# Two chunks of a gated-recurrence layer loaded together, four tokens to a partition, in a kernel that goes on with a wide MLP

## The chip, the cores and the metric

The kernel runs on one core of a Trainium2 chip. The core has five engines with queues of their own: TensorE (PE; PEld are its weight loads), VectorE (DVE), ScalarE (ACT), GpSimd (POOL) and SyncE (SP, which issues most DMAs). Each executes its queue in order; semaphores make one wait for another. The metric is the device time of one execution in microseconds. Steps that an engine takes are called by the kernel's own names throughout (h0.01, qm3.1 and so on); the section on the kernel explains them.

## The reference

For each of 4 batches and 8 heads a state of 48 x 48 runs over 768 tokens. It is decayed by a gate, grows by an outer product, and is read by q:

```
f = 1 / (1 + exp(-f_logit))
for t in range(S):
    state = f[:, :, t, :, None] * state + einsum('bhd,bhe->bhde', k[:, :, t], v[:, :, t])
    y[:, :, t] = einsum('bhd,bhde->bhe', q[:, :, t], state)
```

The result, 3072 tokens x 384, goes through an MLP with 2048 hidden units whose activation is h times cos(h):

```
h = x @ w_in
out = (h * cos(h)) @ w_out
```

## The kernel before

**Chunks and pairs.** The 768 tokens of a batch are cut into chunks of 128. Two neighbouring chunks make a pair of 256 tokens, loaded and prepared together; there are 12 pairs, three to a batch. In a pair's tile one partition holds two neighbouring tokens, e = 0 and 1, for all 8 heads; partitions 0 to 63 are the first chunk (g = 0) and 64 to 127 the second (g = 1). A load (`load`, L294) therefore reads 2 x 48 floats, 384 bytes, in one piece, and 384 KB in one DMA. Heads are worked on four at a time, u = 0 and 1.

**Steps of a pair n** (function `pair`, L311). f, k, q, v are loaded. ACT makes ex (exp(-f_logit)) and ln (log(1 + that), the negative log of the gate). For most pairs POOL adds the two tokens' logs (ad) and PE sums them over the tokens of a chunk by a triangular matrix (cum, L370; its small matmuls with `half` give the totals of each chunk). ACT makes eb and ei, the decays exp(-sum) and exp(+sum). As one sum serves two tokens, the first token of q and the first of k are corrected by one step: fx and fy (ACT) prepare the factors, qa and ka (POOL) apply them. qm and km (L404) multiply q and k by the decays and write them as bf16 side by side in one tile `qk`. vb casts v, and four vt copies lay v out for the matmuls.

The tile qk is then turned, so that head dimensions come to the partitions: for pairs 0 to 4 by PE (tq, tk, L435, sixteen transposing matmuls a pair) and a copy out of PSUM (qkt), for the pairs of `TURN_QK`, 5 to 11, by two DMAs issued from SP (L424). sc (L456) makes the scores k.q, which are masked on the way out of PSUM by am (DVE, L461, 128 x 1024). For the DMA-turned pairs each score matmul is split into two halves, as the turned layout has the two tokens apart. ps (L479) makes the outer products of k and v for the states; st (DVE, L497) adds the state before and sz (DVE, L503) decays the sum. y (L531) is the part of the output from within a chunk, yi that from the state. xe copies the result, already transposed and in bf16, for the MLP.

Pairs 0 and 1 (`HALVES`) are cut into halves of four heads: their f, k and q come in two DMAs each of 192 KB, ex, ln, fx, cum, eb and ei work on half tiles, the log of the two tokens is added by PE (two matmuls instead of one), and qa and ka run partly on DVE.

**The MLP.** `moe` (L566) works on units of 128, 128 and then eleven times 256 tokens; unit m of 256 tokens is pair m - 1. h (L579) is the first matmul into a tile of two PSUM banks, ph, of 1024 columns: h{m}.{j}{s} is half s of tile j. co (ACT, L584) makes the cosine, g (DVE, L561) the product, and o (L595) the second matmul, four steps o{r}.{0..3} to 128 rows; ot copies to SBUF and out stores. The weights arrive in four quarters each, w0.i and w1.i, 768 KB a DMA, and are cast to bf16 by wc on POOL or ACT.

**Order.** Nothing is scheduled at run time or by the compiler: the string `ORDER` (L36) lists every step with its engine's letter (T = PE, S = ACT, V = DVE, G = POOL, Y = SP) and the slot or the PSUM bank of what it writes. An engine's queue is the list of its own steps in that order. A tile name has a number of slots (`SLOTS`), so a load waits until the slot's last readers are done. The steps zf are `ZEROS` = 54 matmuls of a tile of zeros, 128 x 512, whose result nobody reads; they stand in the first part of PE's queue. The steps zqk, zsp, zsz and zvt clear tiles once.

Of the kernel before, what the change touches and what calls it, by code (L numbers as in the profile page):

```python
# [16 lines left out]
C = 128  # L17
# [19 lines left out]
zvt.2:V zsp.1:V zsp.0:G zsz.3:V f0.1:Y0 f0.0:S zqk.0:G k0.0:Y0 ex0.1:S ex0.0:S k0.1:Y ln0.1:S1  # L37
zf0:T0 zf1:T0 zf2:T0 zf3:T0 zf4:T0 zf5:T0 zf6:T0 zf7:T0 zf8:T0 zf9:T0 cum0.1:T0 ln0.0:S cum0.0:T1
fx0.0:S ei0.1:S0 fx0.1:S ei0.0:S ka0.0:V f1.1:Y1 km0.0:G0 f1.0:Y ex1.1:S ka0.1:V zf10:T2 zf11:T2
zf12:T2 zf13:T2 zf14:T2 zf15:T2 zf16:T2 zf17:T2 tk0.0:T2 eb0.1:S0 ex1.0:S ln1.1:S1 ln1.0:S fx1.0:S  # L40
q0.1:Y0 q0.0:Y v0:Y0 fx1.1:S eb0.0:S qa0.1:V zqk.1:V qm0.1:V vb0:S0 f3:Y2 k1.1:Y1 km0.1:V qa0.0:V
zf18:T3 cum1.1:T3 zf19:T4 zf20:T4 zf21:T4 tq0.1:T0 cum1.0:T1 qm0.0:G zsz.2:G eb1.0:S1 vt0.3:S2
k1.0:Y ei1.0:S0 ex3:S zf22:T4 zf23:T4 zf24:T4 zf25:T4 zf26:T4 ps0.1:T4,5 ps0.0:T tk0.1:T v1:Y1 f2:Y0
qkt0.1:V0 eb1.1:S ln3:S0 ei1.1:S ka1.0:G q1.0:Y0 tq0.0:T ka1.1:G km1.1:G0 zvt.1:G vt0.0:S ad3:G1
vt0.1:G q1.1:Y vb1:S1 qkt0.0:V1 vt0.2:G zsz.1:G ex2:S w0.1:Y0 w0.0:Y1 k3:Y0 q3:Y1 w0.3:Y2 ln2:S1
vt1.2:S1 fy3:S zf27:T6 zf28:T6 zf29:T6 zf30:T6 zf31:T6 zf32:T6 sc0.0:T0 sz0.01:V2 sz0.00:V w0.2:Y3
ad2:G0 vt1.0:G km1.0:V vt1.3:G wc0.1:G am0.0:V0 zf33:T6 zf34:T6 yi0:T4 sc0.1:T2 am0.1:V1 st0.11:V
sz0.11:V3 wc0.0:G k2:Y1 zf35:T6 zf36:T6 zf37:T6 zf38:T6 ps1.1:T6,7 tk1.0:T0 ps1.0:T zf39:T1 zf40:T1
zf41:T1 cum3:T1 fy2:S ei3:S0 fx3:S ka3:G eb3:S2 vt1.1:S fx2:S km3.0:G1 qa3:G qm3.0:G km3.1:G qm3.1:G
w1.0:Y0 qa1.0:V st0.10:V qa1.1:V qm1.0:V wc0.2:G ka2:G q2:Y2 tk1.1:T2 zf42:T3 zf43:T3 y0:T3 tq1.0:T  # L50
xe0.1:S0 sz0.10:V st1.00:V st1.01:V qm1.1:V v2:Y1 zf44:T5 zf45:T5 zf46:T5 zf47:T5 zf48:T5 tq1.1:T
cum2:T1 sz1.00:V1 qkt1.0:V0 eb2:S0 xe0.0:S ei2:S1 qkt1.1:V1 km2.0:G0 km2.1:G zf49:T5 sc1.0:T4
sz1.01:V zf50:T0 zf51:T0 sc1.1:T2 h0.01:T0 st1.11:V sz1.11:V2 am1.1:V0 wc1.0:G qa2:G zf52:T6 zf53:T6
h0.00:T co0.0:S0 qm2.1:G am1.0:V1 h1.01:T2 h1.00:T co1.0:S1 y1:T6,4 yi1:T g0.0:V1 xe1.1:V1 st1.10:V
qm2.0:G vb2:G1 sz1.10:V g1.0:V4 w1.2:Y3 xe1.0:S tk3.0:T5 h2.01:T0 tq3.0:T w1.3:Y0 qkt3.0:V0 v3:Y0
# [6 lines left out]
o3.3:T o0.3:T o2.2:T q4:Y2 ps3.0:T4,5 ps3.1:T zsz.0:G vt2.2:G ad4:G0 yi2:T2,3 y2:T vt3.3:G sz3.01:V0
sz3.00:V o1.3:T cum4:T4 v4:Y0 vt3.0:G ad5:G0 fy4:S eb4:S0 st3.11:V fx4:S k4:Y1 fy5:S qa4:G qm4.0:G1
fx5:S ei4:S1 o0.1:T o2.1:T o3.1:T xe2.0:V1 st3.10:V sz3.10:V1 qm4.1:G sz3.11:V xe2.1:V ot2:V0
h3.00:T2 o1.1:T cum5:T0 ei5:S0 eb5:S2 k5:Y0 h3.01:T ot0:V1 vb4:G0 ka4:G y3:T4,5 yi3:T q5:Y1 h3.10:T0
h3.11:T co3.0:S0 xe3.0:V0 xe3.1:V ot1:V2 ot3:V3 co3.1:S2 g3.0:V4 h3.21:T4 h3.20:T co3.2:S1 h4.21:T6
h4.20:T g3.1:V ka5:G km4.0:G co4.2:S0 km4.1:G vt4.1:G2 qa5:G h4.11:T2 h4.10:T g3.2:V co4.1:S2
h4.31:T0 k6:Y2 qm5.1:G0 h4.30:T vt4.0:G vt4.2:G km5.1:G f6:Y1 v5:Y0 v6:Y1 f7:Y0 tq4.0:T4 tq4.1:T5
out3:Y tk4.0:T tk4.1:T co4.3:S1 g4.2:V2 h3.31:T6 h3.30:T qkt4.1:S0 qkt4.0:V1 g4.1:V o5.1:T4 co3.3:S0
o5.2:T o5.0:T o4.1:T5 g4.3:V g3.3:V ps4.1:T0,1 ps4.0:T st4.01:V st4.00:V sc4.1:T2 sc4.0:T6 am4.1:V0  # L70
am4.0:V1 sz4.00:V0 sz4.01:V qm5.0:G vt4.3:G st4.10:V tq5.1:Y2 sz4.10:V2 o5.3:T o4.2:T km5.0:G o4.0:T
o4.3:T ex6:S ln6:S0 vb6:G0 ad6:G0 ex7:S cum6:T2 y4:T3,6 tq5.0:Y3 yi4:T ot5:S3 st4.11:V sz4.11:V
# [116 lines left out]
def describe(nc, cpool, ppool, q, k, v, f_logit, moe_w_in, moe_w_out, out):  # L189
# [528 lines left out]
```

## Time and profile before

| what | value |
|---|---|
| median of 3 runs | 183.36 us (182.91 to 183.54) |
| the profiled execution, its own time | 183.05 us |
| its span, first to last instruction | 181.3 us |
| PE busy | 174.0 us (96%) |
| DVE busy | 138.2 us (76%) |
| ACT busy | 130.7 us (72%) |
| POOL busy | 109.2 us (60%) |
| chain that ended last, share of PE | 80% |
| granted TensorE clock | 0.998 |
| HBM read, written | 25.17 MB, 4.72 MB |

A profile page has six parts: busy time by engine, the span in 40 slices of 4.53 us, the DMA queues, the chain of work that ended last, groups of instructions by line, and the DMA issues. A group's row gives line, engine, operation, tiles and shapes, count, busy time, mean length, and the idle time before with what ended it. Busy PE is not the same as useful PE: the matmuls of zeros count as busy.

### The profile page before, as it was taken

What the parts mean: (1) busy time and instruction counts of PE and PEld (TensorE: products, weight loads), DVE (VectorE), ACT (ScalarE), POOL (GpSimd) and SP (SyncE); (2) the same over time, 40 slices, a digit from 0 to 9 for tenths busy, and PEclk for the clock granted to TensorE, in tenths of its full rate; (3) what the DMA queues carried; (4) which work ended last, traced back from release to release, by engine and by line L of the source; (5) the groups of instructions that cost most, each with busy time, mean ns of one, the idle gap of its engine ahead of it and who ended that gap; (6) DMA issues with size and microseconds to landing.
All of it is one profiled execution on the core that took longest, in us unless ns stands there. A gap on an engine that the chain in (4) does not pass through costs nothing.

```text
span 181.3 us, 5818 instructions
## 1 busy us (share of the span) xinstructions
PE 174.0 (96%) x2464; PEld 124.2 (69%) x2464; DVE 138.2 (76%) x206; ACT 130.7 (72%) x187; POOL 109.2 (60%) x139
## 2 busy tenths in 40 slices
PE   7999788999999999999999999999999999999992
PEld 2555357785677876778657886658788767786661
DVE  5359988898685989897999698689888994466260
ACT  3985988778877999989997899769768452473221
POOL 4229889999969996989755968790799000000000
PEclk9999999999999999999999999999999999999999
DMA  6999999999999945996889999749929400110313
GB/s 141 261 261 263 346 304 318 293 283 281 317 264 241 270 77 128 253 230 133 125 162 317 189 242 253 175 125 244 216 85 197 90 4 0 38 52 4 130 43 130
DMA packets 72282, 33.93 MB, mean 187 GB/s; under 512 B 65344, under 2 KB 70720, under 8 KB 72256
## 3 DMA queue, kind: packets, MB, share of 16 engines
q1 hardware_dynamic: 71584, 33.27, 76.6%
q8 instruction: 19, 0.31, 0.7%
q10 hardware_dynamic: 672, 0.30, 0.6%
q14 instruction: 7, 0.06, 0.1%
HBM read 25.17 MB, written 4.72 MB: 165 GB/s over the span
## 4 chain that ended last, share of the span: by engine, by line
PE 80%; DMA 8%; SPq 5%; DVE 3%; POOL 1%; issue 1%; ACT 1%; POOLq 0%
PE ps L595 35%; PE ps L579 32%; DMA k<-in_k_dram 5%; PE ps L531 5%; SPq L296 3%; PE ps L456 3%; DMA v<-in_v_dram 3%; PE ps L479 2%; DVE g L561 1%; SPq L282 1%; PE ps L435 1%; PE ps L374 1%; DVE am L461 1%; POOL qk L404 1%; POOL k L351 1%
## 5 line engine op out<-in xcount | busy, mean ns | idle before, releaser
L561 DVE TENSOR_TENSOR g<-ps,co 128x1024 bf16<-128x1024 f32 x48 | 61.3, 1311 | 15.8 <-ACT co L584 14.8
L595 PE MATMUL ps<-w_out_bf,g 128*128 128x384 bf16 x384 | 68.9, 326 | 0.0
L579 PE MATMUL ps<-x,w_in_bf 128*128 128x256 bf16 (+1 forms) x624 | 68.2, 264 | 0.6 <-DVE x L197 0.5
L584 ACT ACTIVATE co<-ps,halfpi 128x1024 bf16<-128x1024 f32 x48 | 52.7, 1113 | 20.0 <-PE ps L579 19.8
L579 PEld LDWEIGHTS <-w_in_bf 128*128 128x128 bf16 x624 | 56.3, 98 | 9.3 <-DVE x L197 0.7
L595 PEld LDWEIGHTS <-g 128*128 128x128 bf16 x384 | 36.0, 98 | 21.5 <-issue 0.3
L461 DVE TENSOR_TENSOR am<-ps,pmask 128x1024 bf16<-128x1024 f32 x24 | 28.7, 1218 | 5.0 <-PE ps L456 4.8
L404 POOL TENSOR_TENSOR qk<-k,bi 128x384 bf16<-128x384 f32 x22 | 22.0, 1010 | 5.4 <-ACT bi L391 4.7
L404 POOL TENSOR_TENSOR qk<-q,b 128x384 bf16<-128x384 f32 x21 | 20.9, 1004 | 2.7 <-DVE q L338 2.1
L197 POOL COPY vt<-vb 64x384 bf16<-64x384 bf16 x33 | 16.7, 507 | 1.6
L264 PE MATMUL ps<-zero 128*128 128x512 bf16 x54 | 16.1, 426 | 1.2 <-DVE zero L203 1.2
L503 DVE TENSOR_TENSOR sz<-ps,b 64x192 bf16<-64x192 f32 x40 | 14.1, 353 | 2.5 <-PE ps L479 1.6
L341 POOL TENSOR_TENSOR q<-f,q 128x384 f32<-128x384 f32 x10 | 10.0, 1000 | 8.3 <-DMA q<-in_q_dram 6.1
L363 POOL TENSOR_TENSOR sp<-ls 128x384 bf16<-128x384 f32 x10 | 10.2, 1015 | 7.7 <-ACT ls L333 5.9
L329 ACT ACTIVATE f<-f 128x768 f32<-128x768 f32 (+1 forms) x14 | 10.4, 746 | 4.5 <-DMA f<-in_f_logit_dram 4.4
L351 POOL TENSOR_TENSOR k<-k,f 128x384 f32<-128x384 f32 (+1 forms) x12 | 11.1, 930 | 4.2 <-DMA k<-in_k_dram 4.2
L497 DVE TENSOR_TENSOR ps<-ps,sz 64x192 f32<-64x192 f32 x32 | 11.7, 366 | 1.9 <-PE ps L479 0.8
L197 ACT COPY ot<-ps 128x384 f32<-128x384 f32 (+1 forms) x14 | 6.1, 453 | 8.7 <-PE ps L595 8.7
L197 ACT CAST x<-ps 128x384 bf16<-128x384 f32 x12 | 5.5, 479 | 5.9 <-PE ps L531 5.9
L456 PE MATMUL ps<-qkt 48*64 48x128 bf16 (+1 forms) x304 | 8.7, 219 | 1.0 <-DVE sz L503 0.8
L197 DVE CAST x<-ps 128x384 bf16<-128x384 f32 x12 | 6.4, 552 | 4.0 <-PE ps L531 3.8
L264 PEld LDWEIGHTS <-zero 128*128 128x128 bf16 x54 | 4.9, 105 | 6.1 <-issue 2.2
(64 smaller groups left out, 167.5 us busy)
## 6 DMA issues: line engine op xcount, KB each, us to landing
v<-in_v_dram SPq DMA_DIRECT2D x12, 384.0 KB, 6.0
out_dram<-ot SPq DMA_DIRECT2D x22, 192.0 KB, 2.1
f<-in_f_logit_dram SPq DMA_DIRECT2D x10, 384.0 KB, 6.0
k<-in_k_dram SPq DMA_DIRECT2D x10, 384.0 KB, 6.7
q<-in_q_dram SPq DMA_DIRECT2D x10, 384.0 KB, 6.7
g<-in_moe_w_in_dram SPq DMA_DIRECT2D x4, 768.0 KB, 7.6
g<-in_moe_w_out_dram SPq DMA_DIRECT2D x4, 768.0 KB, 5.8
k<-in_k_dram SPq DMA_DIRECT2D x4, 192.0 KB, 4.5
```

The lines of the kernel that those rows point to most:

```text
L197: (nc.scalar.copy if e == "ACT" else eng(e).tensor_copy)(out=o, in_=i)
L264: G.step(f"zf{i}", ("PE",), lambda e, dump=dump: nc.tensor.matmul(dump.ap, lhsT=zero[:, 0:128], rhs=zero, start=True, stop=True), writes=[ ...
L351: eng(e).tensor_mul(out=w.ap[:, :, 0, :], in0=w.ap[:, :, 0, :], in1=t.ap[:, :, 0, :])
L404: G.step(f"{nm}{n}.{u}", ("POOL", "DVE") if cut else ("POOL",), lambda e, u=u, j=j, src=src, dec=dec: eng(e).tensor_mul(out=qkp[u][j].ap[: ...
L456: nc.tensor.matmul(o[t0:t1, r, 2 * a + g, :].rearrange("p (e n) -> p e n", e=2), lhsT=wide[s, t0 // 64, :] if turned else wide[s].rearrang ...
L461: G.step(f"am{n}.{u}", ("DVE",), lambda e, u=u, sc=sc: nc.vector.tensor_mul(out=am[u].ap.rearrange("p r b n -> p (r b) n"), in0=sc.ap.rear ...
L497: nc.vector.tensor_add(out=view()[s], in0=view()[s], in1=S0.ap[s, :, r, :])
L503: eng(e).tensor_mul(out=new.ap[s, :, r, :].rearrange("p (u a) n -> p u a n", u=2), in0=view()[s].rearrange("p (u a) n -> p u a n", u=2), i ...
L561: nc.vector.tensor_mul(out=o.rearrange("p b (n e) -> p b e n", e=2), in0=ph.ap.rearrange("p (b e n) -> p b e n", e=2, n=64), in1=co.ap.rea ...
L579: nc.tensor.matmul(ph.ap[:, i * T:(i + 1) * T].rearrange("p (g t) -> p g t", t=C), lhsT=w_in_bf[:, kk, f0:f0 + 128], rhs=xa[:, :, kk, :], ...
L584: G.step(f"co{m}.{j}", ("ACT",), lambda e, ph=ph, co=co: nc.scalar.activation(out=co.ap, in_=ph.ap, func=AF.Sin, bias=halfpi), reads=[ph], ...
L595: nc.tensor.matmul(po.ap[:, 0:DM], lhsT=gT.ap[:, j, i * C:(i + 1) * C], rhs=w_out_bf[:, j, :], start=(po.first and j == 4 * s), stop=(po.f ...
```

## The change

Pairs 0 and 1, which are the first 512 tokens of batch 0, are no longer prepared as two pairs. They are prepared together as two tiles t = 0 and 1: tile t holds heads 4t to 4t + 3 of both pairs, with four neighbouring tokens to a partition, pair 0 on partitions 0 to 63 and pair 1 on 64 to 127. A load reads 768 bytes in one piece (`fetch4`), 384 KB a DMA; f0 alone is cut in two.

- The new function `lead4` prepares a tile. ex and ln run on the whole tile. cum sums the logs of all four tokens exactly, by eight matmuls of 192 columns a half tile (masks `incl4` and `strict4`), so that fx, fy, qa and ka are not needed. The decays of one pass cover two of the four tokens (x = 0, 1): eb, ei, qm and km have the form t.x. et makes the totals; tm lays them out for the decay of the states.
- v is spread to where the later matmuls want it by PE (vq, 16 matmuls with slices of the identity) and copied out of PSUM by ACT or DVE (vt0.t, vt1.t), in place of eight copies from SBUF.
- The transposes work on 64 partitions each, as a tile holds two pairs: 16 matmuls of half the size a tile and half, and qkt{w}.{t} copies out pair w of tile t.
- In `pair`, for pairs 0 and 1 (`QUADS`), the scores' mask is `pmask4`, ps takes 32 instead of 64 partitions and twice the matmuls, and the state before is added by PE (si) with slices of the identity, not by DVE (st). sz then covers all 128 partitions by a mask in tm. The product g puts the tokens back with a step of 4 instead of 2.
- `TURN_QK` begins at 4: pair 4 is turned by two DMAs from SP, its scores split into halves.
- `ZEROS` is 25, and `ORDER` is new as a whole. SP's loads begin f0.0, f1, v1, q0, v0, k0, k1, q1, f3, f2, w0.1, w0.3, w0.2, w0.0, k3, w1.2, q3, w1.3, q2, w1.0, v3, k2, f4, w1.1, v2, f5; before they began f0.1, k0.0, k0.1, f1.1, f1.0, q0.1, q0.0, v0, f3, k1.1, k1.0, v1, f2, q1.0, q1.1, w0.1, w0.0, k3, q3, w0.3, w0.2, k2, w1.0, q2, v2, w1.2, w1.3, v3, f4, w1.1 (the other half of f0 is issued by ACT in both).

The other pairs' functions (`lead2`) and the MLP are as they were, cut out of the old `pair`.

```diff
-HALVES = (0, 1)
-TURN_QK = range(5, 12)
+QUADS = (0, 1)
+TURN_QK = range(4, 12)
...
-ZEROS = 54
+ZEROS = 25
...
+        for r in range(4):
+            s = slice(32 * r, 32 * r + 32)
+            nc.vector.tensor_copy(out=incl4[s, s], in_=upper[s, s])
+            nc.vector.tensor_sub(out=strict4[s, s], in0=upper[s, s], in1=ident[s, s])
+            nc.vector.memset(quarter[s, r:r + 1], 1.0)
+            nc.gpsimd.affine_select(out=pmask4[s], in_=pmask4[s], pattern=[[1, 4], [4, 32]], compare_op=ALU.is_ge,
+                                    fill=0.0, base=-r, channel_multiplier=-4)
...
+            tok = src[0, 4 * t + h0:4 * t + h1, 0:4 * C, :] if nc is not None else None
+            G.step(f"{kind}{t}{cut}", ("SP", "ACT") if cut else ("SP",), lambda eg, part=part, tok=tok: eng(eg).dma_start(
+                out=part.ap, in_=tok.rearrange("h (p e) d -> p h (e d)", e=4)), writes=[part])
...
+        def cum(x):
+            for y in range(2):
+                for e in range(4):
+                    nc.tensor.matmul(pc[x].ap[:, HB * y:HB * y + HB], lhsT=incl4 if e <= 2 * x + y else strict4,
+                                     rhs=sp4()[:, e, :, 0:D], start=(y == 0 and e == 0), stop=(y == 1 and e == 3 and x == 1))
...
+        def spread(e):
+            for g in range(2):
+                for u in range(2):
+                    rows = slice(64 * u + 32 * g, 64 * u + 32 * g + 32)
+                    for x in range(4):
+                        nc.tensor.matmul(pv.ap[32 * x:32 * x + 32, 512 * g + HB * u:512 * g + HB * u + HB], lhsT=ident[:, rows],
+                                         rhs=vb4()[:, x].rearrange("p h d -> p (h d)"), start=(u == 0), stop=(u == 1))
...
+                for a in range(2):
+                    for u in range(2):
+                        rows = slice(64 * u, 64 * u + 64)
+                        o = pt[u].ap.bitcast(BF16).rearrange("p (j a g e n) -> p j a g e n", j=2, a=2, g=2, e=4)
+                        nc.tensor.transpose(out=o[:, j, a, :, 2 * x + y, :], identity=ident[rows, rows],
+                                            in_=qkp[x][j].ap[rows, y, 2 * a:2 * a + 2, :].rearrange("p h d -> p (h d)"))
...
+                def carry(e):
+                    for u in us:
+                        first, final = opens(bank(g, u)), closes(bank(g, u))
+                        for i in range(4):
+                            t = slice(32 * i, 32 * i + 32)
+                            nc.tensor.matmul(ps[g].ap[t, at(u):at(u) + HB // 2].rearrange("p (a n) -> p a n", n=D),
+                                             lhsT=ident[:, t], rhs=S0.ap[:, 2 * u:2 * u + 2, i // 2, :], start=first, stop=final)
```

More of the change, by code (lines that the diff above doesn't have):

```diff
@@ L38 @@
[L38 to L55, printed above, removed]
@@ L62 @@
[L62 to L72, printed above, removed]
@@ L115 @@
[L115 to L116 removed]
+zsp.1:G f0.0:Y0 f0.1:S ex0:S zsz.1:V zvt.0:V zqk.1:V zqk.0:V zsp.2:V zsz.0:G zsz.2:G ln0:S1 f1:Y1
+v1:Y0 ex1:S ln1:S2 vb1:G0 zf0:T0 zf1:T0 zf2:T0 zf3:T0 zf4:T0 zf5:T0 zf6:T0 zf7:T0 zf8:T0 zf9:T0
+zf10:T0 zf11:T0 zf12:T0 cum0.1:T0 cum0.0:T1 zf13:T2 vq1:T2 q0:Y0 cum1.0:T4 cum1.1:T5 v0:Y1 eb0.1:S
+et0:S0 eb0.0:S qm0.0:G0 k0:Y0 k1:Y1 q1:Y1 f3:Y2 zvt.1:V qm0.1:V vb0:G1 ei0.0:S0 ei0.1:S1 ei1.0:S2
@@ new lines @@
+et1:S vt0.1:V1 f2:Y0 tm0:G0 km0.0:V tq0.0:T0,1 tq0.1:T vq0:T6 ei1.1:S3 eb1.0:S tk0.0:T km0.1:V
+vt1.1:S0 w0.1:Y0 km1.0:V1 w0.3:Y1 zf14:T4 tk0.1:T qkt0.0:V0 km1.1:G tm1:G1 vt0.0:S eb1.1:S vt1.0:S
+qkt1.0:S1 ex3:S ln3:S0 w0.2:Y2 qm1.0:G zf15:T4 zf16:T4 ps0.0:T2,4 qm1.1:G ad3:G2 w0.0:Y3 fx3:S ex2:S
+ln2:S0 wc0.1:S sc0.0:T6 ps0.1:T sz0.00:V1 sc1.0:T0 sz0.01:V si0.1:T tk1.0:T2,3 ad2:G1 wc0.2:G
+wc0.0:G am1.0:V0 sz0.10:V2 tk1.1:T sz0.11:V am0.0:V1 k3:Y1 w1.2:Y4 ka3:G q3:Y1 tq1.0:T ps1.0:T4,0
+ps1.1:T si1.0:T tq1.1:T w1.3:Y0 q2:Y0 w1.0:Y3 sz1.01:V0 v3:Y1 qkt0.1:V2 qkt1.1:V3 sz1.00:V zf17:T6
```

396 lines of the change are left out of this document (243 added, 153 removed).

## The prediction

> **What bounds the kernel now.** I read three views of the profile in this order: the slices of the page (is an engine full, and from when), the chain of work that ended last (what sets the end), and the timeline of TensorE with the stage windows for the first 35 us, where the change lies.
>
> The slices, and the group of dummy matmuls:
>
> ```profile
> PE   7999788999999999999999999999999999999992
> DMA  6999999999999945996889999749929400110313
> GB/s 141 261 261 263 346 304 318 293 283 281 317 264 241 270 77 128 253 230 133 125 162 317 189 242 253 175 125 244 216 85 197 90 4 0 38 52 4 130 43 130
> ...
> L264 PE MATMUL ps<-zero 128*128 128x512 bf16 x54 | 16.1, 426 | 1.2 <-DVE zero L203 1.2
> ```
>
> PE is full, but 54 of its matmuls multiply zeros. They stand in the first 26 us; the DMA engines are full just there.
>
> The chain, start and length of each piece:
>
> ```profile
> 5.10 5.53 DMA v<-in_v_dram
> ...
> 16.64 8.88 DMA k<-in_k_dram
> ...
> 34.21 2.14 PE ps L579 x24
> ...
> 63.53 0.89 PE ps L435 x16
> ...
> 172.16 5.86 PE ps L595 x36
> ```
>
> Until 34.21 it runs through loads, POOL and DVE. From there to 178.02 it is PE without a hole: 143.8 us of work that no wait lengthens. So only two things can move the end: how early PE comes to productive work, and how much is left then.
>
> The timeline of PE (start, length, count, idle time before), then two stages (PE, PEld, DVE, ACT, POOL busy, clock, DMA share, GB/s):
>
> ```profile
> 1.19 4.45 PE L264 MATMUL ps<-zero 128*128 128x512 bf16 x10 [1.19 <-DVE zero L203]
> ...
> 20.34 1.24 PE L264 MATMUL ps<-zero 128*128 128x512 bf16 x5
> ...
> 24.91 0.84 PE L579 MATMUL ps<-x,w_in_bf 128*128 128x128 bf16 x12
> ```
>
> ```profile
> 8.00:10.00 2.00, 2.00 (x22) 1.25 (x21) 1.60 (x5) 1.82 (x6) 0.19 (x1) 1.00 1.28 262
> ...
> 20.00:22.00 2.00, 1.70 (x13) 0.85 (x13) 1.80 (x6) 1.99 (x6) 1.94 (x3) 1.00 1.02 350
> 22.00:24.00 2.00, 1.14 (x18) 0.63 (x15) 1.93 (x5) 1.96 (x6) 1.94 (x3) 1.00 1.19 301
> ```
>
> The first MoE step h0.01 starts at 24.91. The 384-byte packets of f, k, q, v arrive at 261 GB/s, the weights' packets of 1.5 and 2 KB at 350.
>
> **What is left in the old kernel.** At 24.59 (step sc1.1) PE has 143.8 us from 34.21 on, and before that sc1.1 0.33, h0.01 to h1.00 4 x 0.655, y1 and yi1 0.90, four h2 steps 2.62, and of pair 3 four transposing steps 0.89 and one score step 0.33: 7.7 us (the other 1.9 of that stretch are two dummies and waits). Together 151.5 us. The unit prices are the chain's: an h step 2.62 / 4 (24 matmuls), an o step 0.65, eight score matmuls 0.33.
>
> **Part 1: the loads.** Fourteen DMAs of pairs 0 and 1 become nine, all of 768-byte packets. Old landings fit 3.1 us + bytes / 261 GB/s (v0 10.63, v1 15.14 in the traces, 10.6 and 15.15 by the fit). For 768 bytes no row exists: 261 is one end (1.51 us per 393 KB tensor), 350 the other (1.12 us). 768 is one doubling from either neighbour, so I take the middle, 1.3 us. In SP's new order they land: f0 4.4, f1 5.7, v1 7.0, q0 8.3, v0 9.6, k0 10.9, k1 12.2, q1 13.5; then, at old prices, f3 15.0, f2 16.5, w0.1 18.8, w0.3 21.0, w0.2 23.3, w0.0 25.5, k3 27, w1.2 29.3, w1.3 33.1. f2 waits on SP for the last q product of tile 0 (about 9.9), and all weights stand behind it; three loads are still in flight then, so the queue stays full. [...]
>
> **Part 2: the new path to the first MoE step.** ACT: ex0, ln0, ex1, ln1 at 0.84 each from 4.4 reach 7.8; eb0.1, et0 and eb0.0 (0.49 a row of 384; et, 8 columns, no more than that) 8.9; ei0.0, ei0.1 9.8; it then has twelve steps of 0.3 to 1 us without waiting for data, of which qkt1.0 ends at 14.5. POOL: vb1, then qm0.0 (1.0) 8.9 to 9.9, vb0, tm0, km1.1 12.3 to 13.3. DVE: qm0.1, vt0.1, then k0 is waited for: km0.0, km0.1 (0.53) to 12.0, km1.0 (k1) to 12.8, qkt0.0 (0.67) 13.5. PE: scores 0.33 and ps0.1 0.37 to 14.25. From here DVE's queue is the path: two sz (0.36) 14.97, am1.0 (1.22) 16.2, two sz 16.9, am0.0 18.1, sz1.01 18.5, two qkt 19.8, sz1.00 20.2, am0.1 21.4; y0 on PE 21.9; xe0.0 (0.55) 22.5. So h0.01 starts at 22.5. ACT behind: ex3, ln3, fx3, ex2, ln2 to 18.4, wc0.1 (1.48) 20.3, six steps of 0.5, xe0.1 23.8, wc0.3 25.3. DVE: am1.1 24.7. PE: h1.01 23.85, h0.11 25.35, h0.10, then y1 and yi1 to 27.55; POOL has cast w0.0 by 27.0. **h1.00 starts at 27.55 and no input is late then.**
>
> PE's additions all lie before this: cum 4 x 8 matmuls of 192 columns (0.08 each) and 16 small ones, +1.9 us; vq 0.7; ps twice the matmuls, +0.75; three si of 24 matmuls, together 0.25 to 0.8 (between the row of four-column-group matmuls, 0.016 us, and one after the other); transposes of 64 rows, 64 matmuls at 0.027 to 0.056, against 32 at 0.056: 0 to +1.8. PE waits for DVE in that stretch, so I take nothing for them; without that cover they cost 3 to 6 us. DVE loses six st (2.2 us), four qa, two ka, two net qkt: already in the queue above. The two extra constants' set-up on DVE (12 small operations, 0.06 to 0.7, as rows L217 to L219) end near 5 to 6, before cum0 at 6.4.
>
> **Part 3: pair 4 turned by DMA.** Four transposing steps leave PE, 16 matmuls, 0.89 us (the chain's row at 63.53). Its scores split into twice the matmuls: rows of 16 whole and 32 split both take 0.55 to 0.57, so 0. DVE and ACT each lose one qkt (0.67, 1.01), off the path. SP gains two transposes of 1.9 us issue and 3.3 to landing; behind tq4.0 stand f7 and out2, behind tq4.1 q6 and out3. POOL ends vt2 at 50 (part 4); ad5, vb4, qa4, qm4.0, ka4, km4.0 take it to 55.8, six more to 61.3; landings near 60 and 65. PE wants them at 65 and 68.5 (from 51.4: cum5, sixteen h steps 10.5, three o steps, ps4; then sc4.0 and five o steps): covered by 3 us or more. If that goes, PE waits by what is missing.
>
> **Part 4: new order.** From 27.55 I followed the queues to 53: co and g of eight h tiles run at 1.11 and 1.31 us against PE's 1.31, with four bank pairs of slack; POOL after w0.0's cast (27.0) has thirteen products of 1.0, three casts of 1.47, two vb of 0.82, seven vt of 0.51 and one memset of 0.42: its last vt2 ends at 50.0. PE has twelve h steps 7.9, sixteen o steps 10.4, and of pairs 2 and 3 some 4.9 us before y2: 50.7. So that holds by 0.7; then xe3 comes about 0.5 us late for h4. I add that 0.5. Bounds: 0 (the old order has no wait after 34.21) and 2 us (POOL's margin gone). At the end the last two ot copies run on two engines instead of one after the other: -0.2 (row ACT ot, 0.54 for two).
>
> **Sum.** Left at 27.55: 151.5 - 0.33 (sc1.1, done) - 0.89 - 4 x 0.655 - 0.90 = 146.8. PE ends at 27.55 + 146.8 + 0.5 = 174.8, against 178.02. Tail 3.28 - 0.2; outside the span 183.05 - 181.3 = 1.75. Time 174.8 + 3.1 + 1.75 = **179.6**, 3.4 below the profiled execution's 183.05 (3.8 below the median 183.36).
>
> **The rivals.**
> *Likeliest, 0.54:* as above; by the loads' two ends (k1 1.1 us earlier or 1.4 later, the DVE queue with it) 178.5 to 181.0.
> *POOL late, 0.26:* weight casts wc0.2, wc0.0, wc1.2, wc1.3, wc1.1 stand in POOL's queue, and k, q and vt products of pairs 3 and 2 behind them. For: landings at 24 to 28 and 34 to 40 ran at only 210 to 317 GB/s. At 300, the 6.3 MB of weights take 3 us more, POOL's vt2 ends at 53, and PE waits 1.5 to 2.5: 181.1 to 182.2 (0.16 of it). It ends **slower** only if POOL loses 5 us or more (products of 1.0 stretched by a tenth over 25 us, and the late weights): 184 to 185 (0.10). Against: the old kernel carries the same products with no wait.
> *Clock falls, slower, 0.09:* fewer dummies, and PE idles in pieces up to 1.3 us between 13 and 24. At half clock ps, sc, si and y on the path cost 3 us more and the first 4.45 us of dense work run as the first ten dummies did (445 ns instead of 213), 2.3 us: 179.6 + 5.3 = 184.9; it decides once it costs over 3.4. Against: at 22 to 24 us PE was 57% busy and the clock row stayed 1.00. [...]
> *Nothing gained, 0.05:* loads stay at 261 and every added wait takes the rest: 182.5 to 183.6.
> *Better, 0.06:* loads at the weights' rate and no wait later: 177 to 178.5.
>
> **Chances and range.** 0.3% (0.55 us) is about what a measurement here can tell. Faster 0.54 + 0.16 + 0.06 = 0.76; same 0.05; slower 0.10 + 0.09 = 0.19. The range 177.6 to 183.9 leaves out some 0.03 below and 0.16 above; the likeliest case's own is 178.5 to 181.0.
>
> **What would show it.** Right: 768-byte loads near 300 GB/s from 4 to 13 us; first L579-kind matmul near 22.5; from about 27.5 PE without holes; its end near 175. Wrong: dummies or steps at twice their time after 10 us; PE idle behind POOL between 40 and 55; h0.01 later than 25.9, which alone takes all of the gain.

## The result, and the profile after

The changed kernel takes 190.69 us (median, 190.05 to 192.41) against 183.54 us (182.91 to 184.16) for the old one beside it: a ratio of 1.040, 95% interval 1.034 to 1.046. The forecast was 179.6 us, which is faster. Medians and ranges are of all runs of a kernel; ratios, and the median and range of e2, leave out runs more than 1.5% above its fastest (one to three each in e1, e2, e6, e9, e10 and e11; in e2 it is one of 208.92 us). The profiled execution takes 190.69 us, its span 189.0. Line numbers below are those of the changed kernel: h is L701, g L683, co L706, o L717, am L533, sc L528, y L653, ps L567; copies of every kind are L192. Kernels with added lines are a few to ten lines off.

The slices of the page after, and the group of g:

```profile
PE   7997999666699999999999999999999999999991
DVE  6367655999869689898899987696989884388610
PEclk9997569999999999999999999999999999999998
...
L683 DVE TENSOR_TENSOR g<-ps,co 128x1024 bf16<-128x1024 f32 x48 | 69.4, 1512 | 10.7 <-ACT co L706 10.5
```

The clock and the group of g in the page before:

```profile
PEclk9999999999999999999999999999999999999999
...
L561 DVE TENSOR_TENSOR g<-ps,co 128x1024 bf16<-128x1024 f32 x48 | 61.3, 1311 | 15.8 <-ACT co L584 14.8
```

In the page after, a slice is 4.73 us, and the first is slice 0. Two things are new. TensorE is only two thirds full in slices 7 to 10 (33 to 52 us), where DVE stands at 8 and 9; and the granted clock falls to 0.5 to 0.7 in slices 3 to 5 (14 to 28 us), where it stayed whole before. The group of g says which of the two to look at first: 48 products, as before, but 1512 ns each on average. The tile view of g has the spread (minimum, median, maximum):

```profile
L683 DVE TENSOR_TENSOR g<-ps,co x48: 1285/1314/2548, 31.0 to 177.5; 128x1024 bf16<-128x1024 f32 x48
```

The median, 1314 ns, is the old mean of 1311; the maximum, 2548, is nearly twice that. DVE's timeline shows which ones:

```profile
30.57 0.56 DVE L192 CAST x<-ps 128x384 bf16<-128x384 f32 x1 [4.37 <-PE ps L653]
31.05 18.60 DVE L683 TENSOR_TENSOR g<-ps,co 128x1024 bf16<-128x1024 f32 x8
49.40 0.77 DVE L192 COPY qkt<-ps 128x1024 bf16<-128x1024 bf16 x1
```

Eight products in one row, 18.60 us without a gap, 2.3 us from start to start. They are g of units 0 to 2, the tokens of pairs 0 and 1, and the only ones that write with a step of 4. TensorE fills a pair of banks in 1.31 us (two h steps) and gets it back in 2.3. The chain of what ended last in this stretch, and TensorE's timeline (start, length, count, idle time before and who ended it):

```profile
31.05 12.98 DVE g L683 x6
44.03 0.79 issue
44.81 3.06 DVE g L683 x2
47.88 1.52 issue
49.40 0.77 DVE qkt L192
50.17 1.14 DVE am L533
```

```profile
33.56 1.47 PE L701 MATMUL ps<-x,w_in_bf 128*128 128x256 bf16 x12 [0.35 <-DVE g L683]
35.87 1.47 PE L701 MATMUL ps<-x,w_in_bf 128*128 128x256 bf16 x12 [0.84 <-DVE g L683]
38.18 1.50 PE L701 MATMUL ps<-x,w_in_bf 128*128 128x128 bf16 x24 [0.84 <-DVE g L683]
40.50 1.47 PE L701 MATMUL ps<-x,w_in_bf 128*128 128x256 bf16 x12 [0.82 <-DVE g L683]
42.80 0.38 PE L499 MATMUL ps<-ident,qk 128*128 128x128 bf16 x4 [0.83 <-DVE g L683]
...
45.10 0.61 PE L499 MATMUL ps<-ident,qk 128*128 128x128 bf16 x8 [1.26 <-DVE g L683]
...
47.40 0.40 PE L528 MATMUL ps<-qkt 48*128 48x128 bf16 x8 [0.17 <-DVE g L683]
...
51.34 0.40 PE L528 MATMUL ps<-qkt 48*128 48x128 bf16 x8 [1.48 <-DVE am L533]
```

These holes sum to 6.59 us. In the last the same DVE queue is late by way of qkt and am. Where the old kernel had a stretch of TensorE without a hole, there is now a stretch of DVE without one.

The other suspect, in the stage windows (PE, PEld, DVE, ACT, POOL busy, clock, DMA share, GB/s):

```profile
14.00:16.00 2.00, 1.73 (x67) 1.23 (x69) 1.16 (x3) 0.93 (x2) 2.00 (x4) 1.00 1.10 279
16.00:18.00 2.00, 1.20 (x79) 1.17 (x81) 2.00 (x4) 1.94 (x4) 1.14 (x2) 0.67 0.95 309
18.00:20.00 2.00, 2.00 (x38) 0.92 (x30) 1.62 (x4) 1.91 (x3) 0.78 (x2) 0.50 0.98 336
```

It falls at 16.7 us and stays at 0.50 to 26.9. h0.01 starts at 24.87 and h1.00 at 30.39; the forecast had 22.5 and 27.55, the old kernel ran h0.01 at 24.91. So there are two candidates for 11.1 us of miss: the write step of g, and a half clock with a late start.

### The profile page after: what moved, and what is told of

It reads as the page before. It is cut to its first block, busy times and chain, and to the rows that moved or that the text cites. A ratio compares the mean times of both kernels' runs of the same rounds, so it can differ in the third digit from the quotient of the medians.

```text
span 189.0 us, 6097 instructions
## 1 busy us (share of the span) xinstructions
PE 174.8 (93%) x2611; PEld 127.1 (67%) x2611; DVE 141.9 (75%) x209; ACT 131.1 (69%) x180; POOL 107.6 (57%) x139
## 4 chain that ended last, share of the span: by engine, by line
PE 76%; DVE 12%; DMA 4%; issue 2%; SPq 2%; ACT 1%; POOL 1%; DVEq 0%; POOLq 0%; ACTq 0%
PE ps L717 31%; PE ps L701 30%; DVE g L683 8%; PE ps L653 5%; DMA k<-in_k_dram 4%; PE ps L528 4%; PE ps L567 3%; DVE am L533 2%; SPq L319 2%; PE ps L270 2%; PE ps L451 1%; DVE qkt L192 1%; DVE sz L602 1%; POOL sp L443 1%; PE ps L499 0%
## 5 line engine op out<-in xcount | busy, mean ns | idle before, releaser
L683 DVE TENSOR_TENSOR g<-ps,co 128x1024 bf16<-128x1024 f32 x48 | 69.4, 1512 | 10.7 <-ACT co L706 10.5
L701 PE MATMUL ps<-x,w_in_bf 128*128 128x256 bf16 (+1 forms) x624 | 67.5, 267 | 2.9 <-DVE g L683 2.8
L717 PE MATMUL ps<-w_out_bf,g 128*128 128x384 bf16 x384 | 67.4, 326 | 0.0
L701 PEld LDWEIGHTS <-w_in_bf 128*128 128x128 bf16 x624 | 57.2, 99 | 11.2 <-issue 4.0
L706 ACT ACTIVATE co<-ps,halfpi 128x1024 bf16<-128x1024 f32 x48 | 52.7, 1114 | 16.8 <-PE ps L701 11.3
L717 PEld LDWEIGHTS <-g 128*128 128x128 bf16 x384 | 36.1, 98 | 22.2
L533 DVE TENSOR_TENSOR am<-ps,pmask 128x1024 bf16<-128x1024 f32 x24 | 28.9, 1222 | 7.0 <-PE ps L528 6.8
L469 POOL TENSOR_TENSOR qk<-k,bi 128x384 bf16<-128x384 f32 x20 | 19.8, 1005 | 0.6
L443 POOL TENSOR_TENSOR sp<-ls 128x384 bf16<-128x384 f32 x10 | 10.0, 999 | 14.8 <-PE ps L528 9.4
L192 POOL COPY vt<-vb 64x384 bf16<-64x384 bf16 x30 | 15.1, 503 | 1.7
L435 POOL TENSOR_TENSOR k<-k,f 128x384 f32<-128x384 f32 x10 | 10.0, 1001 | 8.4 <-issue 4.9
L192 ACT COPY ot<-ps 128x384 f32<-128x384 f32 (+1 forms) x13 | 6.0, 466 | 12.0 <-PE ps L717 11.9
L623 DVE TENSOR_TENSOR sz<-ps,b 64x192 bf16<-64x192 f32 x32 | 11.2, 354 | 3.1 <-PE ps L567 2.3
L192 ACT CAST x<-ps 128x384 bf16<-128x384 f32 x13 | 6.2, 482 | 10.2 <-PE ps L653 10.0
L192 DVE CAST x<-ps 128x384 bf16<-128x384 f32 x11 | 6.0, 553 | 7.6 <-PE ps L653 7.4
L270 PE MATMUL ps<-zero 128*128 128x512 bf16 x25 | 10.2, 553 | 1.3 <-DVE zero L198 1.3
L192 DVE COPY ot<-ps 128x384 f32<-128x384 f32 (+1 forms) x13 | 6.5, 503 | 6.3 <-PE ps L717 4.5
L528 PE MATMUL ps<-qkt 48*64 48x128 bf16 (+1 forms) x320 | 9.4, 223 | 1.7 <-DVE am L533 1.5
L617 DVE TENSOR_TENSOR ps<-ps,sz 64x192 f32<-64x192 f32 x26 | 9.5, 366 | 1.1 <-PE ps L567 0.2
L528 PEld LDWEIGHTS <-qkt 48*64 48x64 bf16 (+1 forms) x320 | 6.4, 106 | 4.9 <-issue 2.7
```

The source lines that it names most:

```text
L192: (nc.scalar.copy if e == "ACT" else eng(e).tensor_copy)(out=o, in_=i)
L270: G.step(f"zf{i}", ("PE",), lambda e, dump=dump: nc.tensor.matmul(dump.ap, lhsT=zero[:, 0:128], rhs=zero, start=True, stop=True), writes=[ ...
L443: G.step(f"ad{n}", ("POOL",), lambda e: eng(e).tensor_add(out=sp.ap[:, 0, :, 0:D], in0=soft.ap[:, :, 0, :], in1=soft.ap[:, :, 1, :]), read ...
L469: G.step(f"{nm}{n}.{u}", ("POOL",), lambda e, u=u, j=j, src=src, dec=dec: eng(e).tensor_mul(out=qkp[u][j].ap[:, :, :, 0:D], in0=swap(src.a ...
L528: nc.tensor.matmul(o[t0:t1, r, 2 * a + g, :].rearrange("p (e n) -> p e n", e=E), lhsT=wide[s, t0 // 64, :] if turned else wide[s].rearrang ...
L533: G.step(f"am{n}.{u}", ("DVE",), lambda e, u=u, sc=sc: nc.vector.tensor_mul(out=am[u].ap.rearrange("p r b n -> p (r b) n"), in0=sc.ap.rear ...
```

## The experiments

Theory 1: a product that writes bf16 with a step of four elements is slower than one with a step of two, and that alone is the loss. Theory 2: the clock. The old kernel beside e1 to e4 took 183.26 us, beside e5 to e8 183.55, beside e9 to e11 183.33.

**e1, the changed kernel with g's old step.**

```diff
-gate(gv, ph, co, T, 4 if n in QUADS else 2)
+gate(gv, ph, co, T, 2)
```

> The changed kernel with the product g of units 0, 1 and 2 written with a step of 2 elements, as all others are, in place of 4. It leaves out part of the restoring of the token order, so the rows of the first 512 tokens come out permuted; everything else is the same. Theory 'step': the eight g from 31 us on took 18.6 us in a row, 2.32 each, against 1.31 for the rest, and PE waited for them; then g goes back to 1.31 each, VectorE's row of eight shrinks by some 8 us, and the time falls by 6 to 8 us, to 183 to 185. Rival 'clock': the TensorE clock at half from 16.7 to 27.2 us is what made the kernel late; then the row of g was only late by its start, and the time falls by no more than 2 us, to 188.5 or more.

Measured: 183.37 us (182.28 to 185.3), ratio 0.999 (0.996 to 1.002). The tile view of g:

```profile
L683 DVE TENSOR_TENSOR g<-ps,co x48: 1283/1310/1336, 32.9 to 171.7; 128x1024 bf16<-128x1024 f32 x48
```

One number in the code carries 7.3 us, and the rest of the change comes out at nothing, not at a gain. In this profile, too, the clock is at half for a while (22.8 to 29.7 us).

**e2, the reverse: the old kernel with a step of 4 for the same units.**

```diff
-gate(gv, ph, co, T)
+gate(gv, ph, co, T, 4 if n < 2 else 2)
```

> The kernel before with one thing of the change: the product g of units 0, 1 and 2 written with a step of 4 (rows of the first 512 tokens permuted). Theory 'step': each of these eight g takes 2.3 us instead of 1.31, and the old kernel, whose VectorE is nearly full from 28 to 42 us, gets slower by 4 to 8 us, 187.5 to 191.5. Rival 'clock': a longer g is absorbed, 183 to 185, as the clock of the old kernel does not fall.

Measured: 191.07 us (190.94 to 191.42), ratio 1.043 (1.040 to 1.045), with a granted clock of 0.997 in the profile. The tile view of g:

```profile
L561 DVE TENSOR_TENSOR g<-ps,co x48: 1293/1315/2525, 28.0 to 181.2; 128x1024 bf16<-128x1024 f32 x48
```

The old kernel loses 7.8 us by the same step, with old loads, old order and full clock. Between e1 and e2 the cause of the slowdown is settled.

**e3, the step moved to where it is cheap.** For units 0 to 2 g writes in order, and the four stores of pairs 0 and 1 put the rows back.

```diff
+nc.vector.tensor_mul(out=o, in0=ph..., in1=co...)
-eng(e).dma_start(out=out[r0:r0 + C, c0:c1], in_=oc.ap)
+eng(e).dma_start(out=rows.rearrange("(n e) c -> e n c", e=E), in_=oc.ap)
```

> The changed kernel with the product g of units 0, 1 and 2 written in order, and the token order restored by the DMA that stores the rows (1536 bytes a row as before), so nothing is left out. Theory 'step': g costs 1.2 to 1.3 us as the products am of the same size do (1.22); time 182.5 to 184.5, a little under the run with a step of 2. Rival 'clock': 188.5 or more.

Measured: 183.23 us (182.31 to 184.48), ratio 0.9996 (0.997 to 1.002). The groups of g, with and without reordering:

```profile
L686 DVE TENSOR_TENSOR g<-ps,co 128x1024 bf16<-128x1024 f32 x40 | 50.7, 1312 | 11.3 <-ACT co L716 11.2
...
L684 DVE TENSOR_TENSOR g<-ps,co 128x1024 bf16<-128x1024 f32 x8 | 9.5, 1220 | 0.4 <-ACT co L716 0.2
```

In TensorE's timeline the holes are gone, apart from one of 0.34 behind POOL at 54.03:

```profile
24.08 1.30 PE L711 MATMUL ps<-x,w_in_bf 128*128 128x128 bf16 x12
...
29.19 8.09 PE L711 MATMUL ps<-x,w_in_bf 128*128 128x128 bf16 x96
...
54.03 0.32 PE L451 MATMUL ps<-sp,incl 128*128 128x384 bf16 x1 [0.34 <-POOL sp L443]
...
166.31 10.56 PE L727 MATMUL ps<-w_out_bf,g 128*128 128x384 bf16 x64
```

From h1.00 at 29.19 to TensorE's end at 176.87 it is 147.7 us; the forecast had 146.8 + 0.5. So what was to be left at h1.00 is right to 0.4 us. This profiled execution took 182.41 us, 2.8 more than the forecast: 1.6 lie before h1.00, 0.4 behind it, and 0.7 in the tail (3.8 us in place of 3.1), where the last two ot copies still run one after the other (ACT to 177.28, DVE from 177.30). The median of this kernel is 0.8 higher still, in a range of 2.2.

**e4 and e6, the clock.** Six more dummies between 14.8 and 17.2 us, in the changed kernel (e4) and in e3 (e6).

```diff
-sz0.01:V si0.1:T tk1.0:T2,3 ... tq1.0:T ps1.0:T4,0
+sz0.01:V zf25:T2 si0.1:T zf26:T2 zf27:T3 zf28:T2 tk1.0:T2,3 ... tq1.0:T zf29:T0 zf30:T1 ps1.0:T4,0
```

> The changed kernel with six more matmuls of zeros, in PE's holes between 14.8 and 17.2 us, just before the clock row fell to 0.5. Theory 'step': the clock row stays at 1.00 or falls later, the first g starts 1 to 2 us earlier, but the row of eight long g stays: 188.5 to 190.5. Rival 'clock': with the clock up the kernel gets back 5 us or more, 186 or less.

> e3 (g in order, order restored by the store) with the six dummies of e4. Of the 3.6 us by which e3 missed the forecast of 179.6, theory 'clock' says that half clock between 16 and 27 us costs about 1.5 to 2, as PE's steps y0, si, cum, sc and the first h stand on the path there: 181.3 to 182. Rival 'supply': PE has holes inside steps that no engine explains (1.1 and 2.1 us in e1, 1.8 in e4), they come with or without the clock: 182.8 to 183.8, no change.

e4: 190.53 us (190.09 to 191.19), ratio 1.039. The same windows of e4, and DVE's row:

```profile
16.00:18.00 2.00, 1.85 (x37) 0.85 (x37) 2.00 (x5) 1.94 (x4) 1.23 (x2) 1.00 0.90 286
18.00:20.00 2.00, 2.00 (x85) 1.19 (x84) 1.47 (x3) 1.91 (x4) 0.77 (x2) 1.00 0.88 292
```

```profile
30.44 18.60 DVE L683 TENSOR_TENSOR g<-ps,co 128x1024 bf16<-128x1024 f32 x8
```

The dummies kept the clock whole until TensorE's end, and the time stayed: theory 2 is out for this kernel. The row of g starts only 0.6 us earlier, where 1 to 2 was expected, because TensorE now stands 1.81 us before 23.20 without a wait that the profile names. e6: 183.07 us (181.41 to 184.26), ratio 0.996 (0.994 to 0.998). That lies in the rival's range; it is the first kernel whose interval is below 1, by 0.4%, and the interval of e3 overlaps it. So the dummies are worth somewhere from 0 to 1 us once g is out of the way. What the clock alone is worth is not separated by this: in e6 it held until 23.6 us and fell then, behind a stop of the kind of e4, which e9 is about.

**e5, the price list of the step.** Units of pairs 2 to 8 write, or read, in other orders (1, 2, 4, 8, 16 elements; then in order, with ph and co read at steps of 32 and 64).

```diff
+E = {3: 1, 4: 2, 5: 4, 6: 8, 7: 16, 8: -4, 9: -2}.get(m, 1 if E == 4 else E)
```

> A price list, not a version. The kernel of e3, but the product g of units 3 to 7 is written with a step of 1, 2, 4, 8 and 16 elements, and that of units 8 and 9 is written in order while PSUM and the cosine are read with a step of 32 and 64 elements (so the rows of units 3 to 7 come out permuted). Theory 'write step': steps of 1 and 2 cost 1.22 and 1.31 us, 4 costs 2.5, and 8 and 16 as much or more; read steps cost nothing, about 1.3. Rival 'short runs': what costs is that a run in the innermost dimension has 32 elements instead of 64; then each further halving adds about as much again (8: 3.5 to 5 us, 16: 6 us or more), and the reads in other orders, with runs of 4 and 2, are dearer still.

The kernel takes 211.76 us. g in the tile view, stretch by stretch: step 1, step 4 (its maximum is a step 8), three of step 16 with two of step 8, and reading at 32:

```profile
L689 DVE TENSOR_TENSOR g<-ps,co x4: 1210/1213/1215, 62.2 to 66.7; 128x1024 bf16<-128x1024 f32 x4
...
L691 DVE TENSOR_TENSOR g<-ps,co x5: 2439/2468/4777, 80.1 to 90.2; 128x1024 bf16<-128x1024 f32 x5
...
L691 DVE TENSOR_TENSOR g<-ps,co x5: 4717/4737/4931, 115.8 to 133.6; 128x1024 bf16<-128x1024 f32 x5
L686 DVE TENSOR_TENSOR g<-ps,co x2: 1852/1912/1972, 138.0 to 139.9; 128x1024 bf16<-128x1024 f32 x2
```

Writing costs 1.21 us at step 1, 1.31 at 2, 2.47 at 4, 4.7 to 4.9 at 8, and 4.5 to 4.7 at 16. So the price nearly doubles from 2 to 4 and again from 4 to 8, and at 16 it is no higher: over these five steps it goes with the distance between two writes from 2 to 8 elements (4 to 16 bytes), and no further. The rival, shorter runs of what is read, foresaw 6 us or more at 16, and falls there. Reading is not always free, against the expectation: 1.9 us at step 32, but 1.2 at step 64.

**e7, the wide packets alone.** e3 with each load of pairs 0 and 1 in two DMAs of 384-byte packets.

```diff
-eng(eg).dma_start(out=part.ap, in_=tok.rearrange("h (p e) d -> p h (e d)", e=4))
+[eng(eg).dma_start(out=part.ap[:, :, 2 * D * i:...], in_=tok...[:, :, 2 * D * i:...]) for i in range(2)]
```

> e3 with each load of pairs 0 and 1 cut into two DMAs of two tokens, so packets of 384 bytes as in the kernel before. Theory 'packets': 4 to 12 us go at 261 GB/s instead of 320, k1 lands 1.5 to 2 us later, and the first MoE step with it: 184.5 to 185.5. Rival 'hidden': the path to the first MoE step is set by VectorE's and ScalarE's queues and the clock, so 0 to 0.7 us, 183.2 to 184.

Measured: 183.27 us, ratio 0.998 (0.996 to 1.000). Windows of e7, then the same of e3:

```profile
6.00:8.00 2.00, 1.46 (x22) 1.45 (x22) 0.25 (x1) 1.97 (x3) 0.18 (x1) 1.00 1.21 272
8.00:10.00 2.00, 1.75 (x42) 1.38 (x39) 0.59 (x1) 1.69 (x6) 1.63 (x2) 1.00 1.23 265
```

```profile
6.00:8.00 2.00, 1.88 (x25) 1.67 (x25) 0.23 (x1) 1.97 (x5) 0.50 (x1) 1.00 1.03 296
8.00:10.00 2.00, 1.63 (x36) 1.47 (x36) 1.03 (x2) 1.26 (x4) 1.51 (x2) 1.00 1.09 340
```

The wide packets arrive at 296 and 340 GB/s in these windows and the narrow ones at 272 and 265, as foreseen, and it makes no difference in time: the rival 'hidden' held.

**e8, can the old kernel have the cheap g everywhere?** All 48 products in order, and all 26 stores put rows back, two by two.

```diff
-nc.vector.tensor_mul(out=o.rearrange("p b (n e) -> p b e n", e=2), in0=..., in1=...)
+nc.vector.tensor_mul(out=o, in0=ph..., in1=co...)
-eng(e).dma_start(out=out[r0:r0 + C, c0:c1], in_=oc.ap)
+eng(e).dma_start(out=rows.rearrange("(n e) c -> e n c", e=2), in_=oc.ap)
```

> The kernel before with all 48 products g written in order and the token order restored by the stores. Theory 'PE bounds from 34 us on': g falls from 1.31 to 1.22, 4.3 us off VectorE in all, but no wait for g stands on the chain, so 0 to 0.6 us faster: 182.7 to 183.4. Rival: the g row is near the path around 28 to 42 us and at the end, 1 us or more faster.

Measured: 241.03 us, ratio 1.31, far from both expectations. g did become 1224 ns; what is lost stands in the waits (total, times, longest):

```profile
ACT ot L197 <- DMA out_dram<-ot: 47.4, 6, 16.5
```

The copy to an output tile waits up to 16.5 us for the tile's store. Four stores of the form (4, 32 rows) did no harm in e3; 26 of the form (2, 64 rows) cost 57 us. Number and form both differ, and the DMA view tells them apart: where such a store runs alone in e8 (168.8 to 170 us) the 16 DMA engines are busy to 1 tenth and move some 50 GB/s; in e3 (64.3 to 65.3 us) to 2 or 3 tenths, at some 100 GB/s; an unpermuted store of the old kernel (158.2 to 158.6 us) to 6 tenths or more, at 230 to 460. So each permuting store is slow, the form of 2 twice as slow as that of 4, and in e3 no copy waits for one. Of 16 engines 1 tenth is the time of some two and 2 to 3 tenths that of three to five, an estimate from these shares; no view lists the engines one by one.

**e9, stops with nothing to wait for.** In e1, e3, e4 and e6 TensorE stands idle before 22 to 24 us with the mark "issue", that is, with nothing that the profile shows it waiting for. e6 again, with its first nine dummies cut into eight pieces each: 63 matmuls more in the queue before 6 us, on the same columns.

```diff
-matmul(dump.ap, lhsT=zero[:, 0:128], rhs=zero, ...)
+[matmul(dump.ap[:, c:c + w], lhsT=zero[:, 0:128], rhs=zero[:, c:c + w], ...) for c in range(0, 512, w)]
```

> The kernel of e6, in which each of the first nine dummy matmuls of 512 columns is issued as eight of 64 columns: the same columns and the same results, but 63 matmuls more in TensorE's queue before about 6 us. In e6, e1, e3 and e4 TensorE stood still before 22 to 24 us with nothing to wait for in the profile, and each time the stop ended 2.4 to 2.6 us after the start of a 16 KB packet of the instruction queue (packets at 20.0, 21.2, 19.4, 20.8; ends 22.42, 23.79, 21.89, 23.20); the packets stood some 6.5 us apart while the loads ran. Theory 'instruction supply' (a packet is a block of 128 matmuls with their weight loads, and the next one comes no sooner than some 6.4 us after the last began to be used): the packets move to other times, 63 matmuls earlier in the program, the stop moves with them to before the ps, si and tq steps of pair 1 (16 to 20 us) and again to around y0 and si1.1, 1 to 3 us in all; h0.01 starts at 25 to 27 in place of 23.95, and the time is 184.0 to 187, from 183.1. Rival 'the step itself' (the stop belongs to yi0 or sits there by chance): packets or not, the stop stays before yi0, h0.01 at 23.5 to 24.5, time 182.7 to 183.5.

TensorE's timeline of e6, then all of e9's stops, with the row ahead of the second:

```profile
22.42 0.27 PE L653 MATMUL ps<-qkt,sz 128*32 128x128 bf16 x5 [1.80 <-issue]
```

```profile
19.61 0.37 PE L568 MATMUL ps<-vb,qk 32*64 32x48 bf16 x23 [0.58 <-issue]
...
24.63 0.56 PE L712 MATMUL ps<-x,w_in_bf 128*128 128x128 bf16 x7
26.08 0.44 PE L712 MATMUL ps<-x,w_in_bf 128*128 128x128 bf16 x5 [0.89 <-issue]
...
32.28 1.91 PE L712 MATMUL ps<-x,w_in_bf 128*128 128x256 bf16 x16 [0.21 <-issue]
```

The stop inside yi0 is gone, and there are three others, one of them in the middle of h0.01. Counted row by row, the first stands exactly 63 matmuls earlier in the program than the stop of e6, which is what was added ahead of it; 128 matmuls lie between the first and the second, and 128 between the second and the third. Packets of the instruction queue, 16 KB each, start at 17.3, 23.7 and 29.8, and the stops end 2.3 to 2.5 us after them; the long stops of e1, e4 and e6 end 2.4 to 2.6 us after such a packet, those of e10 and e11 2.1 to 2.5. That points to the supply of instructions: 128 matmuls with their 128 weight loads are 256 instructions, and the page of the changed kernel counts 20 such packets (0.33 MB) to 2611 matmuls with 2611 weight loads, 20.4 times 256. In this stretch the packets come 6.1 to 6.4 us apart. Whether the loads that run meanwhile set that distance, no run here separates. The longest of these stops is 2.24 us (e11). The time is 183.46 us (182.15 to 186.34), ratio 0.9995, and h0.01 starts at 24.63: the stops add up to about as much as before (1.68 us), so the forecast of 184 to 187 and of 25 to 27 was wrong, while the stop moved by the 63 matmuls as its theory said.

**e10, ACT's order between y0 and h1.00.** e6 with w0.3's cast ahead of eb2, xe0.1 right behind y0, and the four dummies among the first h steps gone.

```diff
-fy3:S am0.1:V2 y0:T6 xe0.0:V0 ... eb2:S1 xe0.1:S wc0.3:S
+fy3:S wc0.3:S am0.1:V2 y0:T6 xe0.0:V0 xe0.1:S ... eb2:S1
-h0.01:T6 zf21:T0 h1.01:T0 zf22:T3 zf23:T3 zf24:T3 h0.11:T4
+h0.01:T6 h1.01:T0 h0.11:T4
```

> The kernel of e6 with ACT's cast of w0.3 moved ahead of eb2 and its xe0.1 right behind y0, and without the four dummies zf21 to zf24 between h0.01 and h0.11. In e6 h1.00 began at 29.96, and h0.01 and h1.01 ran at half the clock (24 to 27 us). Theory 'what is left of the miss lies between y0 and h1.00': four dummies of 0.43 at half clock and xe0.1's half microsecond go, h1.00 starts at 28.0 to 29.0, time 181.6 to 182.6. Rival 'w0.0 is the limit' (it lands at 26.1 and POOL's cast ends at 27.65) and 'stops for instructions take it back': h1.00 at 29.3 or later, time 182.8 to 183.3.

Measured: 182.96 us (181.91 to 185.17), ratio 0.996 (0.9945 to 0.998), the same as e6. Its timeline:

```profile
22.93 0.27 PE L653 MATMUL ps<-qkt,sz 128*32 128x128 bf16 x5 [1.59 <-issue]
...
24.35 4.48 PE L711 MATMUL ps<-x,w_in_bf 128*128 128x128 bf16 x48
...
30.01 4.24 PE L711 MATMUL ps<-x,w_in_bf 128*128 128x128 bf16 x49
```

The four h steps now stand back to back, but a stop of 1.59 is there again and behind it the clock is at half from 24.7 to 28.1 us, so they take 4.4 us in place of 2.6, and h1.00 starts at 30.0 as in e6. The rival that the stops take it back held; w0.0 was not the limit, as POOL's cast of it ended at 27.8.

**e11, pair 4 turned by TensorE again.** e6 with the turn of pair 4 undone.

```diff
-TURN_QK = range(4, 12)
+TURN_QK = range(5, 12)
-o4.2:T ... ps4.1:T sc4.0:T2
+o4.2:T tq4.0:T2 tk4.0:T tq4.1:T3 tk4.1:T qkt4.0:V0 qkt4.1:S2 ... ps4.1:T o5.3:T sc4.0:T2
```

> The kernel of e6 with pair 4 turned by PE again: four transposing steps and two copies (DVE 0.67, ACT 1.0) stand before ps4.0, its score matmuls are whole, and SP's two transposes are gone; o5.3 is moved ahead of sc4.0 as cover. Theory of Part 3 (four transposing steps of PE are 0.89 us on a path without holes): 0.9 slower than e6, 183.7 to 184.3. Rival 'hidden': ACT and DVE are what PE waits for around 60 to 70 us anyway, so within 0.4 of e6, 182.7 to 183.5. Third: PE also waits for the copies, 1.2 to 2 slower than e6, 184.3 to 185.1.

Measured: 186.18 us (184.53 to 188.61), ratio 1.014 (1.009 to 1.019), more than any of the three expectations. TensorE's timeline in the profiled execution, of 185.35 us:

```profile
68.19 1.06 PE L499 MATMUL ps<-ident,qk 128*128 128x128 bf16 x16
...
76.74 0.32 PE L451 MATMUL ps<-sp,incl 128*128 128x384 bf16 x1 [0.16 <-POOL sp L443]
77.70 0.32 PE L451 MATMUL ps<-sp,incl 128*128 128x384 bf16 x1 [0.55 <-POOL sp L443]
```

TensorE ends at 179.94, in e6 at 177.07. Of the 2.9 us, 0.7 lie before h1.00 (a stop of 2.24), 0.89 are the transposes, and 0.71 are two new waits: ACT waits 1.7 us for the transposes, its ex6, ln6 and ex7 are late by it, so POOL's sums are, and then cum7 and cum6. So in this order the turn by DMA is worth at least the 0.89 of Part 3, and more, because it also frees ACT's queue. The other 0.6, and the wide scatter of this kernel, stay open.

## Why the prediction was wrong

**The step that failed** is in Part 4: "co and g of eight h tiles run at 1.11 and 1.31 us against PE's 1.31, with four bank pairs of slack". The price of g was taken from the 48 products of the old kernel, which all write with a step of 2. That these eight write with a step of 4 was in the diff and in the account of the change, but not among the edits that were costed: no bound, no rival. Measured, they take 2.5 us each, 2.3 from start to start (1.31 in e1, 1.22 in e3). Eight times 1.0 more than TensorE's 1.31 is 8 us, which the four bank pairs of slack could not hold; TensorE's timeline shows 6.6 us of holes, e1 7.3 and e2 7.8 us of time. It is a mis-sized term of the sum and no fault of the mechanism: DVE was to keep pace with TensorE at the same 1.31 us, and so a rise of that row beyond the slack reaches the end.

**The other terms.** From 190.69 to 179.6 is 11.1 us: about 7.3 for the step (e1) and 3.8 for the rest, of which e3's profiled execution shows 2.8.
- *What is left at h1.00* (146.8 + 0.5): right, 147.7 in e3. POOL's last vt2 ends at 51.30, 1.4 us ahead of y2, where 0.7 was counted. The one hole is another, 0.34 before cum5, behind POOL's ad5.
- *Part 1, the loads*: right in size (296 to 340 GB/s), but worth nothing (e7). k1 landed half a microsecond late, at 12.7.
- *Part 2, the path to h1.00*: h0.01 came 2.4 us late and h1.00 2.8 in the changed kernel, 1.6 each in e3. Two steps of the working failed. One is "y0 on PE 21.9; xe0.0 (0.55) 22.5": in TensorE's queue si1.1, cum2 and sc1.1 stand between y0 and h0.01 as well. From the end of am0.1 to h0.01 1.1 us were counted, and in e3 it is 2.7, of which 0.2 is a stop; with the clock whole, in e6, y0 and these steps take 1.5. So some 0.4 are the steps left out and some 1.0 the half clock. The other is "PE waits for DVE in that stretch": in the changed kernel DVE waits for TensorE, 0.38 before sz1.01 and 0.79 before am0.1, which ends at 22.5 in place of 21.4. That it ends at 21.4 in e3 is partly luck, as DVE's queue was half a microsecond ahead of the forecast and then waited 0.49 for TensorE's scores. From h0.01 to h1.00 it is 5.1 us in e3, as foreseen.
- *The dummies and "I take nothing" for TensorE's additions*: the matmuls are small, so they cost little time (64 of ps take 0.69 us in e6), but each is an instruction. Before h0.01, at 24.9 us in both, the old kernel has 258 matmuls and the changed one 403, and e9 points to the supply of these as what runs out. It varies from execution to execution: the changed kernel, e1 and e3 give TensorE the same queue, and their profiles show 0, 3.2 and 0.2 us of such stops.
- *Part 3*: its 0.89 is borne out (e11).

**The rivals.** "Clock falls" was given 0.09 and 184.9 us. Its mechanism came: half clock from 16.7 to 27 us. It did not decide: e2 loses 7.8 us with the clock whole, and e1 and e3 are at the old time with the clock at half for 6.8 us. From the first matmul to the fall the longest hole of TensorE is 0.8 us. The 213 ns a dummy of its sum stand in no row: in the old profile one dummy more takes 0.22 us (six 1.46, five 1.24), against 0.445 in the first ten. "POOL late" stayed at 0.34 us (e3). "Nothing gained", at 182.5 to 183.6, is the time of e1 and e3, the change without the step, but not for its reason: the loads did not stay at 261 GB/s, and the earlier h0.01 that they were to bring was eaten by TensorE's steps, its clock and its stops between am0.1 and h0.01.

## What to carry to other kernels

Of an instruction that keeps its line, shape and operands, compare the access pattern too: a group's mean holds for the step that it was measured with, and here a bf16 write at a step of four elements cost nearly twice one at a step of two (2.47 against 1.31 us, e5). Where a tensor must be reordered once, ask which of its stations does it for least; here four stores took it over without a loss that can be seen, while 26 stores of another shape cost 57 us. And when a change replaces a few large matmuls by many small ones while loads run, count instructions as well as microseconds.

## What was not expected of the hardware

- The step prices of DVE for a bf16 result of 128 x 1024: 1.21, 1.31, 2.47, 4.7 to 4.9 and 4.5 to 4.7 us at steps of 1, 2, 4, 8 and 16 elements (e5).
- TensorE's instructions came in packets of 16 KB, which fit 128 matmuls with their weight loads; in the changed kernel they start at 13.25, 20.15, 26.80 and 32.25 us, 5.5 to 6.9 us apart, in e9 6.1 to 6.4. TensorE stood still for 0.2 to 2.2 us at a time, which the view of idle time calls "issue" (e1, e3, e4, e6, e9 to e11).
- Stores that permute rows with an outer dimension of 2 ran at some 50 GB/s and held their tiles up to 16.5 us (e8).
- The clock fell to half at 16.7 us after the change, with TensorE 81% busy in the 3.4 us before, on small matmuls and with holes of at most 0.8 us. Its low stretches last 3.4 us (e6, e10, e11), 6.8 (e1, e3) or 10.2 (the changed kernel). Busy time alone does not tell when it falls. In the 3.4 us before the fall TensorE was 34 to 53% busy in e1, e6, e10 and e11, with a stop in that stretch, but 73% in e3; in e2 the clock stood through a stretch of 53% (27.6 to 31.0 us). What else counts is open.
